# Reordering VectorE's and GpSimd's side work in the first pair of batches: gates ahead of conversion, weight sums in pieces, two weight matrices parked in DRAM

## The chip, the cores and the metric

The kernel runs on one core of a Trainium2 chip. The metric is the device time of the program in microseconds, from the median of several runs. All arithmetic is in fp32; the matmul engine is called TensorE or PE, the others VectorE (DVE), ScalarE (ACT), GpSimd (POOL) and SyncE (SP), which issues nearly all DMAs.

## The reference

```python
def _attn_ref(x, state):                # x (8, 8, 512, 64), state (8, 8, 32, 64)
    scores = scale * x @ state^T;  a = softmax(scores);   xread = a @ state
    scores2 = scale * state @ x^T; a2 = softmax(scores2); sread = a2 @ x
    return concatenate([xread, sread], axis=2)

def _moe_ref(x, w_in, w_out):           # x (4352, 512), w_in (512, 2048), w_out (2048, 512)
    h = x @ w_in
    g = h * np.cos(h)
    return g @ w_out

x = attn_out.transpose(0, 2, 1, 3).reshape(B * S, H * D)
```

There are eight batches. Each gives 512 token rows and 32 state rows to the second block. The two weight matrices arrive as float64, so the kernel converts them on the chip with integer operations.

## The kernel before, in words

The kernel walks through 80 **steps**; a step is one tile of 128 hidden columns of one batch (16 per batch), and the last 16 steps are the state rows of all batches. Two batches are a **pair** (32 steps, `PERIOD`). For a tile, TensorE makes the hidden values `h` in PSUM (`hidden`, L490); then comes the **gate** h*cos(h) in four parts: `gate` (ScalarE, L560, rounds h), `gate2` (VectorE, L563, the remainder), `gate3` (ScalarE, L566, the sine), `gate4` (VectorE, L580, the product, into a slot of `g_all`). In the first pair `h` has two PSUM buffers, so the matmuls of tile t+2 wait for `gate4` of tile t. The output product g @ w_out follows: for the first two rows of tiles plainly (L633), and for all others by a seven-product scheme on half matrices, two levels deep (L745), which needs sums of weights and sums of gated tiles.

`g_all` holds 12 **quads** of four tiles (128 x 2048 floats each) and a ring of four weight blocks. Quads 5 to 8 hold the four quarters A11, A12, A21, A22 of w_out, 9 to 11 are landing places of raw float64 data, quad 4 (`TEMPS`) takes GpSimd's temporaries. A quad whose content is used up goes to the list `quads_free`, and a tile or a sum takes one from its head.

What happens in the first pair beside the gates:

- **Conversion.** `convert(i, parts)` turns load i of 18 from float64 to fp32: "1" and "2" on ScalarE (L243, L246), "b" a shift on VectorE (L249), "c" an and/xor on VectorE (L252), "d" an add on GpSimd (L257), "f" fetches the next load. The table `conv_at` gives a step to each load; b, c, d follow one step later. The last load is finished in step 16. `e`, the exponents, lies in `aS_all`.
- **Weight sums.** For each of seven products the four quarters of a matrix are combined: `inner_weights` makes four sums on GpSimd (L671) and sends eight blocks of 256 KB to DRAM (`blocks_kept`). The matrices are A22, A11 and A12 themselves and four sums of them: SQ = A21+A22 (GpSimd), A21 = A11-A21 (VectorE), A22 = SQ-A11 (GpSimd) and SQ = A12-A22 (VectorE), all in L1092. Steps 15 to 27 hold this list, and A12 has its turn in step 50. Later, `fetch_block` on SP reads a block into the ring, three stages ahead of its use.
- **Outer sums.** Row2-row0 of the gated tiles goes to VectorE (L692), for this pair in steps 25 to 28.
- **Attention of the next batches**, placed by `plan(b)`: six lists per step (`pe`, `x_act`, `y_act`, `x_dve`, `y_dve`, `z_act`), which `go(0)` to `go(5)` issue at fixed places around the four parts of the gate.

The order on each engine is the order of the program, and every engine and the SP queue work in order. `first_pair` writes it out for steps 0 to 27, `later_pair` for the others. At the end of a step come the stores (`later`), `weights_at`, `outer_at` and `sums_at` of that step. In the later pairs tiles are gated two at a time (128x1024), and the hidden values of every token tile but those of the last quarter come from the seven-product scheme too: `sw_sums` (GpSimd, L523) and `halves` (VectorE, L509, into `aS_all`) prepare that.

Of the kernel before, what the change touches and what calls it, by code (L numbers as in the profile page):

```python
# [10 lines left out]
F32 = mybir.dt.float32  # L11
I32 = mybir.dt.int32
U32 = mybir.dt.uint32
ALU = mybir.AluOpType
# [8 lines left out]
def kernel(  # L23
# [8 lines left out]
    nc = tc.nc  # L32
# [4 lines left out]
    P = 128  # L37
# [38 lines left out]
    def quad(n):  # L76
        return g_all[:, QT * n:QT * n + QT]

    def matrix(n):
        return quad(n).rearrange("p t (u d) -> p (t u) d", d=HD)  # L80
# [6 lines left out]
            for i in range(NB)]  # L87
    spare = ctx.enter_context(tc.tile_pool(name="spare", bufs=1,
                                           space=bass.MemoryType.DRAM))
    blocks_kept = spare.tile([7, 8, P, QT * P], F32)  # L90

    xT = consts.tile([P, NK, S], F32)
    x_b = consts.tile([P, NC, H, D], F32)
# [170 lines left out]
    class Attention:  # L264
# [115 lines left out]
            self.exp2()  # L380

        def inverse(self, v):
            w = v.rearrange("p (a b) -> p b a", b=2)
            nc.vector.tensor_scalar(w, w, 1e-9, None, op0=ALU.add)
            nc.vector.reciprocal(v, v)
# [273 lines left out]
        m = m.rearrange("p (k i) (m d) -> p m k i d", k=2, m=2)  # L659
        return m[:, 0, 0], m[:, 0, 1], m[:, 1, 0], m[:, 1, 1]  # L660

    def inner_weights(which, m, temps=TEMPS):

        m11, m12, m21, m22 = quarters(m)
        t1, t2, t3, t4 = [quad(temps)[:, n].rearrange("p (i d) -> p i d", d=P)
                          for n in range(4)]
        for o, x1, x2, op in ((t1, m21, m22, ALU.add),
                              (t2, t1, m11, ALU.subtract),
                              (t3, m11, m21, ALU.subtract),
                              (t4, m12, t2, ALU.subtract)):  # L670
            nc.gpsimd.tensor_tensor(o, x1, x2, op=op)  # L671
        for n, block in enumerate((m11, m12, t4, m22, t1, t2, t3, m21)):
            nc.sync.dma_start(
                out=blocks_kept[which, n].rearrange("p (i d) -> p i d", d=P),
                in_=block)

    stage_list = []

# [279 lines left out]
    def plan(b):  # L958
# [12 lines left out]
        def early(b, s):  # L971
            if b == 1:
                pairs(s[0], b, "tokens", "tokens_kept", 0)
                pairs(s[1], b, "tokens", "tokens_kept", 2)
            else:
                for k in range(NK):
                    to = (x_dve, y_dve)[k % 2]
                    to[s[k // 2]].append((b, "tokens_turned", k))
            pe[s[2]].append((b, "scores"))
            x_dve[s[2]].append((b, "max1"))  # L980
            x_dve[s[3]].append((b, "spread1"))
            y_dve[s[3]].append((b, "shift"))
            if b == 1:
                x_dve[s[4]].append((b, "max2"))
                y_act[s[4]].append((b, "exps"))
            else:
                y_dve[s[4] - 1].append((b, "max2"))
                z_act[s[4]].append((b, "exps"))
            if b == 1:
                x_dve[s[5]].append((b, "sums"))  # L990
                y_dve[s[5]].append((b, "spread1"))
                x_dve[s[6]].append((b, "norm1"))
            else:
                y_dve[s[4]].append((b, "sums1"))
                x_dve[s[5]].append((b, "spread2"))
                y_dve[s[5]].append((b, "norm1"))

        def late(b, s):
            pairs(s[0], b, "turn", "turn_kept", 0)
            pe[s[1]].append((b, "reads", 0))  # L1000
            pe[s[2]].append((b, "reads", 1))
            x_dve[s[2]].append((b, "keep"))
            if len(s) > 3:
                turned(b, s[3])
# [65 lines left out]
    for n in range(B // 2):  # L1070
        end = n == B // 2 - 1
        for r, engine, o, x1, x2, half in (
                ((25, 26), dve, 0, 2, 0, 0), ((27, 28), dve, 0, 2, 0, 1),
                ((31, 31), pool, 2, 3, 2, 0), ((33, 33), dve, 0, 3, 0, 0),
                ((34, 34 + (not end)), dve, 0, 3, 0, 1),
                ((35, 36), dve, 2, 3, 2, 1),
                ((38 - end,) * 2, pool, 1, 1, 0, 0),
                ((39 - end,) * 2, pool, 1, 1, 0, 1)):
            for i in range(2):
                outer_at[PERIOD * n + r[i]].append(  # L1080
                    (engine, n, o, x1, x2, half, i))

# [2 lines left out]
                     for r in (o, x1, x2)]  # L1085
        sub(engine, o, x1, x2)

    def weight_sum(engine, o, x1, x2, op):
        n = 1 if engine is pool else 2
        for i in range(0, QT, n):  # L1090
            o_, x1_, x2_ = [quad(q)[:, i:i + n] for q in (o, x1, x2)]
            engine.tensor_tensor(o_, x1_, x2_, op=op)  # L1092

    def last_weights():
        temps = quads_free.pop(0)
        inner_weights(1, a12, temps)
        weights_at[53].append(lambda: quads_free.extend([A12, temps]))

    A11, A12, A21, A22, SQ = 5, 6, 7, 8, 11
    add_, sub_ = ALU.add, ALU.subtract  # L1100
    for at_, what in (
            (15, lambda: quads_free.append(10)),
            (16, lambda: inner_weights(2, a22)),
            (17, lambda: quads_free.append(9)),
            (17, lambda: weight_sum(pool, SQ, A21, A22, add_)),
            (18, lambda: inner_weights(3, matrix(SQ))),
            (18, lambda: weight_sum(dve, A21, A11, A21, sub_)),
            (19, lambda: inner_weights(0, a11)),
            (20, lambda: weight_sum(pool, A22, SQ, A11, sub_)),
            (21, lambda: inner_weights(5, matrix(A21))),  # L1110
            (22, lambda: inner_weights(4, matrix(A22))),
            (23, lambda: quads_free.append(A11)),
            (24, lambda: weight_sum(dve, SQ, A12, A22, sub_)),
            (25, lambda: quads_free.append(A21)),
            (25, lambda: inner_weights(6, matrix(SQ))),
            (27, lambda: quads_free.extend([A22, SQ, TEMPS])),
            (50, last_weights)):
        weights_at[at_].append(what)

    n_stages = 0  # L1120

# [17 lines left out]
    def first_pair(step, t):  # L1139
# [5 lines left out]
        if step == 0:  # L1145
            hidden(all_tiles[1])
            warm(3, acc[0])
            gate(t)
            gate2(t)
            convert(3, "bcdf")  # L1150
            convert(4, "1")
            go(0)
        else:
            go(0)
            if step == 5:
                states(1, side_banks[0])
            gate(t)
            gate2(t)
            if step == 3:
                warm(4, acc[0])  # L1160
                part(0, "products", 1, SIDE)
            go(1)
            go(3)
            if step == 1:
                convert(4, "bcdf")
            elif last >= 0:
                convert(last, "bcdf")
            if conv >= 0 and not todo[1]:
                convert(conv, "1")
        gate3(t)  # L1170
        go(5)
        if step == 3:
            part(0, "products_kept", 1, SIDE)
        gate4(t)
        if conv >= 0 and todo[1] and step > 0:
            convert(conv, "1")
        if step == 6:
# [129 lines left out]
```

## Time and profile before

| | before |
|---|---|
| median of 3 runs | 764.57 us (764.47 to 765.46) |
| span of the profiled run | 762.7 us |
| granted TensorE clock, mean | 0.990 |
| bytes read from and written to HBM | 87.03 and 23.59 MB |

The largest groups of the page, by engine (line, engine, operation, operands, count; busy us, mean ns; then idle time ahead of them and what ended most of it):

```profile
L692 POOL TENSOR_TENSOR g_all<-g_all 128x512 f32<-128x512 f32 x256 | 336.4, 1345 | 108.3 <-PE o L745 62.8
L745 PE MATMUL o<-g_all 128*128 128x256 f32 x1456 | 345.2, 382 | 4.4 <-POOL g_all L692 2.4
L490 PE MATMUL h<-aT,sw 128*128 128x512 f32 x224 | 108.8, 610 | 12.8 <-DVE g_all L580 12.1
L692 DVE TENSOR_TENSOR g_all<-g_all 128x1024 f32<-128x1024 f32 x40 | 56.7, 1433 | 0.1
L671 POOL TENSOR_TENSOR g_all<-g_all 128x512 f32<-128x512 f32 x28 | 37.7, 1371 | 12.2 <-DMA blocks_kept<-g_all 11.6
```

The mean of a pipelined matmul is longer than its share of the time: four 128x512 matmuls of one tile (L490) take 1.73 us from the start of the first to the start of what follows. The numbers of a row are sums over the whole run, so a row says how much there is, and the place is found in the timeline.

### The profile page before, as it was taken

To read this page: it belongs to the slowest core of one execution; us is meant where nothing else is said; L and a number is where in the kernel's file an instruction comes from. 1 tells how busy PE (TensorE), PEld (TensorE's weight loads), DVE (VectorE), ACT (ScalarE), POOL (GpSimd) and SP (SyncE) were. 2 spreads that over 40 slices of the span, in tenths; PEclk is the share of its full clock that TensorE was granted. 3 is DMA by queue.
4 is the path that set the end of the run, shared out by engine and by line. 5 is a ranking of instruction groups with operands and counts; after the bars stand their busy time and mean duration, and the time that the engine had idled before them with its cause. 6 is when DMAs were issued, how large, how long until landed. Compare 5 with 4: busy or idle time off the path is not lost.

```text
span 762.7 us, 10471 instructions
## 1 busy us (share of the span) xinstructions
PE 721.2 (95%) x3552; PEld 507.0 (66%) x3552; DVE 490.1 (64%) x683; ACT 330.9 (43%) x538; POOL 516.9 (68%) x480
## 2 busy tenths in 40 slices
PE   8998887779999999999999999999999999999998
PEld 3443322337777876677768876687778767888886
DVE  5768786783886757686866667759746446264650
ACT  3877962633454445434363445343634432211110
POOL 2344267779799895378998952479989534799600
PEclk9999998999999999999999999999999999999999
DMA  8495359679422685477225843672224456445661
GB/s 248 166 275 173 125 118 273 223 243 188 117 86 75 139 239 144 106 140 170 76 77 113 190 109 93 134 193 84 75 69 120 111 164 156 116 144 192 180 156 40
DMA packets 210356, 111.32 MB, mean 146 GB/s; under 512 B 158272, under 2 KB 173120, under 8 KB 210304
## 3 DMA queue, kind: packets, MB, share of 16 engines
q1 hardware_dynamic: 209216, 110.14, 55.3%
q8 instruction: 28, 0.46, 0.3%
q10 hardware_dynamic: 960, 0.39, 0.2%
q14 instruction: 24, 0.20, 0.1%
q0 software_dynamic: 128, 0.13, 0.1%
HBM read 87.03 MB, written 23.59 MB: 145 GB/s over the span
## 4 chain that ended last, share of the span: by engine, by line
PE 60%; POOL 20%; DVE 5%; DMA 5%; issue 4%; ACT 3%; SPq 1%; POOLq 0%; DVEq 0%; ACTq 0%
PE o L745 31%; POOL g_all L692 13%; PE h L490 10%; PE h L540 9%; POOL g_all L671 4%; PE at L328 3%; PE at L846 2%; DMA g_all<-blocks_kept 2%; POOL swS_all L523 2%; PE at L425 1%; DMA blocks_kept<-g_all 1%; POOL sw L523 1%; DMA x_b<-in_x_dram 1%; PE o L921 1%; PE o L846 1%
## 5 line engine op out<-in xcount | busy, mean ns | idle before, releaser
L692 POOL TENSOR_TENSOR g_all<-g_all 128x512 f32<-128x512 f32 x256 | 336.4, 1345 | 108.3 <-PE o L745 62.8
L745 PE MATMUL o<-g_all 128*128 128x256 f32 x1456 | 345.2, 382 | 4.4 <-POOL g_all L692 2.4
L745 PEld LDWEIGHTS o<-g_all 128*128 128x128 f32 x1456 | 273.9, 191 | 65.3 <-issue 19.2
L563 DVE TENSOR_TENSOR q_all<-q_all,h 128x1024 f32<-128x1024 int32 (+1 forms) x88 | 85.4, 970 | 58.7 <-ACT q_all L560 58.6
L490 PE MATMUL h<-aT,sw 128*128 128x512 f32 x224 | 108.8, 610 | 12.8 <-DVE g_all L580 12.1
L566 ACT ACTIVATE q_all<-q_all,halfpi 128x1024 f32<-128x1024 f32 (+1 forms) x88 | 84.3, 958 | 61.8 <-DVE q_all L563 61.7
L580 DVE TENSOR_TENSOR g_all<-h,q_all 128x1024 f32<-128x1024 f32 (+1 forms) x88 | 85.7, 974 | 34.6 <-ACT q_all L566 32.3
L560 ACT ACTIVATE q_all<-h 128x1024 int32<-128x1024 f32 (+1 forms) x88 | 73.5, 835 | 74.3 <-DVE g_all L580 32.3
L490 PEld LDWEIGHTS h<-aT,sw 128*128 128x128 f32 x224 | 41.5, 193 | 59.8 <-issue 32.1
L549 DVE TENSOR_TENSOR h<-h,sums_all 128x256 f32<-128x256 f32 x72 | 30.9, 429 | 63.7 <-PE h L540 49.0
L692 DVE TENSOR_TENSOR g_all<-g_all 128x1024 f32<-128x1024 f32 x40 | 56.7, 1433 | 0.1
L540 PE MATMUL h<-aS_all,swS_all 128*128 128x256 f32 x144 | 45.8, 400 | 7.3 <-POOL swS_all L523 5.5
L750 ACT COPY o<-o 128x256 f32<-128x256 f32 x26 | 9.3, 357 | 88.0 <-PE o L745 88.0
L540 PE MATMUL h<-aT,sw 128*128 128x256 f32 x144 | 44.7, 392 | 2.9 <-DVE g_all L580 2.5
L671 POOL TENSOR_TENSOR g_all<-g_all 128x512 f32<-128x512 f32 x28 | 37.7, 1371 | 12.2 <-DMA blocks_kept<-g_all 11.6
L257 POOL TENSOR_TENSOR w_in<-w_in,aS_all 128x1024 int32<-128x1024 int32 (+1 forms) x10 | 19.3, 1927 | 37.6 <-DVE w_in L252 22.3
L540 PE MATMUL h<-aS_all,sw 128*128 128x256 f32 x144 | 43.5, 384 | 0.0
L540 PEld LDWEIGHTS h<-aS_all,swS_all 128*128 128x128 f32 x144 | 25.5, 191 | 26.6 <-issue 7.8
L756 ACT COPY o<-sums_all 128x256 f32<-128x256 f32 x26 | 9.8, 378 | 74.0 <-PE o L745 74.0
L603 DVE SCALAR_TENSOR_TENSOR held<-o,held 128x512 f32<-128x512 f32 x40 | 27.1, 680 | 21.3 <-PE o L745 20.8
L461 ACT COPY sw<-at 128x512 f32<-128x512 f32 x50 | 26.8, 588 | 31.3 <-PE at L328 31.3
L257 POOL TENSOR_TENSOR g_all<-g_all,aS_all 128x1024 int32<-128x1024 int32 x8 | 18.9, 2363 | 29.3 <-DVE g_all L252 22.0
(112 smaller groups left out, 869.1 us busy)
## 6 DMA issues: line engine op xcount, KB each, us to landing
g_all<-blocks_kept SPq DMA_DIRECT2D x202, 256.0 KB, 2.8
blocks_kept<-g_all SPq DMA_DIRECT2D x56, 256.0 KB, 3.0
g_all<-in_moe_w_out_dram SPq DMA_DIRECT2D x8, 1024.0 KB, 5.1
out_dram<-ot SPq DMA_DIRECT2D x128, 64.0 KB, 2.0
g_all<-in_moe_w_in_dram SPq DMA_DIRECT2D x6, 1024.0 KB, 5.9
xT<-in_x_dram SPq DMA_DIRECT2D x96, 64.0 KB, 3.0
x_b<-in_x_dram SPq DMA_DIRECT2D x24, 256.0 KB, 4.9
x_b<-in_x_dram SPq DMA_DIRECT2D x16, 128.0 KB, 4.4
```

The source lines that it names most:

```text
L257: nc.gpsimd.tensor_tensor(bits, bits, e, op=ALU.add)
L490: nc.tensor.matmul(out=t.hp, lhsT=t.lhs(i), rhs=t.rhs(i), start=(i == 0), stop=(i == t.kn - 1))
L540: nc.tensor.matmul(out=out_, lhsT=w, rhs=r, start=start, stop=True, skip_group_check=True)
L549: nc.vector.tensor_tensor(o, h2[:, LO], sums_all[:, 0], op=ALU.add)
L560: nc.scalar.activation(t.q.bitcast(I32), t.hp, func=ACTF.Copy, bias=0.25)
L563: nc.vector.tensor_tensor(t.q, t.q.bitcast(I32), t.hp, op=ALU.subtract)
L566: nc.scalar.activation(t.q, t.q, func=ACTF.Sin, bias=halfpi, scale=-TWO_PI)
L580: nc.vector.tensor_tensor(g, t.hp, t.q, op=ALU.mult)
L603: nc.vector.scalar_tensor_tensor(out=out.t[:, ch], in0=bank, scalar=TWO_PI, in1=b.t[:, ch], op0=ALU.mult, op1=ALU.add)
L671: nc.gpsimd.tensor_tensor(o, x1, x2, op=op)
L692: engine.tensor_tensor(o[:, i:i + n], x1[:, i:i + n], x2[:, i:i + n], op=ALU.subtract)
L745: nc.tensor.matmul(out=o, lhsT=ring[(self.first + k) % NB][:, i], rhs=g[:, i], start=(start and i == 0), stop=(i == QT - 1), skip_group_ch ...
```

## The change

All of it concerns the first pair, except the two parked matrices.

1. In `first_pair`, `gate4` is issued ahead of the conversion: "b" stays ahead of `gate3` only where the step's `x_dve` list is empty, and "c", "d", "f" follow `gate4`.
2. The attention of batch 2 is spread: its maxima, exponentials, sums and normalisation are put one list or one step apart, and the second exponential comes one step after the first.
3. The sums row2-row0 of the first pair are made tile by tile (128x512) in steps 17 to 24, right after the tile, and VectorE's two weight sums are cut in four pieces each (steps 19 to 21 and 22 to 24).
4. The sums of A11 go to steps 9 to 12, one per step. GpSimd's temporaries have two homes, `TEMPS` and `aS_all`, in turns.
5. A22 (step 16) and A12 (step 22) are copied to DRAM (`kept`) and come back in steps 44 and 48 into a quad from the free list; their sums are made in steps 46 and 50. A12's quad is free from step 28 on. Before, A22 had its sums in step 16 and A12 held its quad to step 53.
6. The stores of `inner_weights` are put on `stores_due`, and so are issued at the head of the next step.

```diff
+    kept = spare.tile([2, P, QT * S], F32)
...
-        for n, block in enumerate((m11, m12, t4, m22, t1, t2, t3, m21)):
...
+        def send():
+            for n, block in enumerate((m11, m12, t4, m22, t1, t2, t3, m21)):
...
+        if 3 in pieces:
+            stores_due.append(send)
...
+            elif b == 2:
+                x_dve[s[4] - 1].append((b, "max2"))
+                z_act[s[4] - 1].append((b, "exp1"))
+                x_dve[s[4]].append((b, "sums1"))
+                z_act[s[4]].append((b, "exp2"))
+                x_dve[s[5]].append((b, "inverse", None))
+                y_dve[s[5]].append((b, "spread1"))
+                x_dve[s[5] + 1].append((b, "norm1"))
...
-                ((25, 26), dve, 0, 2, 0, 0), ((27, 28), dve, 0, 2, 0, 1),
+                (n and (25, 26), dve, 0, 2, 0, 0),
+                (n and (27, 28), dve, 0, 2, 0, 1), ((31, 31), pool, 2, 3, 2, 0), ((33, 33), dve, 0, 3, 0, 0),
...
+    def late_weights(step):
+        if step == 44:
+            late_quads.append(quads_free.pop(0))
+            move(late_quads[0], 0, False)
+        elif step == 46:
+            late_quads.append(quads_free.pop(0))
+        elif step == 48:
+            move(late_quads[0], 1, False)
+        elif step == 53:
+            quads_free.extend(late_quads)
+        if step in (46, 50):
+            q, temps = late_quads
+            inner_weights(2 if step == 46 else 1, matrix(q), quad(temps))
...
-            (16, lambda: inner_weights(2, a22)),
+            (16, lambda: move(A22, 0, True)),
...
-            (18, lambda: weight_sum(dve, A21, A11, A21, sub_)),
-            (19, lambda: inner_weights(0, a11)),
...
+            (22, lambda: move(A12, 1, True)),
...
-            (24, lambda: weight_sum(dve, SQ, A12, A22, sub_)),
...
+    for i in range(QT):
+        weights_at[9 + i].append(lambda i=i: inner_weights(
+            0, a11, temps[0], (i,)))
+        weights_at[(19, 20, 21, 21)[i]].append(lambda i=i: weight_sum(
+            dve, A21, A11, A21, sub_, (i,)))
+        weights_at[(22, 23, 24, 24)[i]].append(lambda i=i: weight_sum(
+            dve, SQ, A12, A22, sub_, (i,)))
+    for i in range(NH):
+        weights_at[17 + i].append(lambda i=i: first_outer_sum(i))
+    for step in (44, 46, 48, 50, 53):
+        weights_at[step].append(lambda step=step: late_weights(step))
...
-            if step == 1:
-                convert(4, "bcdf")
-            elif last >= 0:
-                convert(last, "bcdf")
+            if last >= 0 and not todo[3]:
+                convert(last, "b")
...
         gate4(t)
+        if last >= 0:
+            convert(last, "bcdf" if todo[3] else "cdf")
```

## The prediction

> **What bounds the kernel now.** I read the page first (who is busy), then the list of waits of the matmul queue (what it stands still for), then a table of engine time in stretches (where), and last the timeline around the largest waits (why).
>
> ```profile
> span 762.7 us, 10471 instructions
> PE 721.2 (95%) x3552; PEld 507.0 (66%) x3552; DVE 490.1 (64%) x683; ACT 330.9 (43%) x538; POOL 516.9 (68%) x480
> ...
> PE   8998887779999999999999999999999999999998
> ...
> POOL 2344267779799895378998952479989534799600
> PEclk9999998999999999999999999999999999999999
> DMA  8495359679422685477225843672224456445661
> ```
>
> TensorE is the bound: busy in tenths of 9 from slice 10 on (a slice is 19 us), and only the first ten slices, 0 to 190 us, have holes. That is the first pair of batches, steps 0 to 31. So a change there can win at most the holes, and a change in the second pair can win next to nothing but can lose. The waits of the matmuls between 20 and 190 us (us in total, times, longest):
>
> ```profile
> PE h L490 <- DVE g_all L580: 12.1, 9, 2.5
> PE at L328 <- DVE xT L310: 5.6, 1, 5.6
> PE h L540 <- POOL swS_all L523: 4.7, 1, 4.7
> PE o L745 <- DMA g_all<-blocks_kept: 1.3, 2, 0.9
> PE at L287 <- DMA x_b<-in_x_dram: 1.0, 2, 0.5
> ```
>
> Three causes carry 22.4 us: the gate product (L580) that releases the PSUM buffer of a tile two steps on, one long wait for a VectorE transpose, and one for GpSimd's weight sums. By stretches (stretch, length, then busy us of PE, PEld, DVE, ACT, POOL, granted clock, DMA share, GB/s):
>
> ```profile
> 80.00:100.00 20.00, 16.12 (x83) 7.34 (x82) 14.79 (x22) 17.78 (x24) 6.76 (x3) 1.00 0.50 130
> 100.00:120.00 20.00, 15.04 (x67) 4.89 (x65) 13.26 (x15) 7.85 (x13) 15.93 (x12) 1.00 0.52 133
> 120.00:140.00 20.00, 17.45 (x52) 5.96 (x52) 13.90 (x21) 8.50 (x13) 15.85 (x12) 0.83 0.92 253
> 140.00:160.00 20.00, 15.10 (x76) 6.66 (x76) 17.19 (x24) 10.00 (x18) 12.22 (x10) 0.91 0.67 213
> 160.00:180.00 20.00, 14.91 (x54) 9.76 (x47) 12.56 (x17) 5.61 (x12) 19.61 (x21) 0.91 0.88 220
> ```
>
> PE lacks 3.9, 5.0, 2.6, 4.9 and 5.1 us here, and its clock falls to 0.83 and 0.91: busy time is stretched as well. ACT is near full from 80 to 100 us, POOL from 100 on. The timeline shows the 5.6 us wait being made:
>
> ```profile
> 113.97 5.91 POOL L1092 TENSOR_TENSOR g_all<-g_all 128x512 f32<-128x512 f32 x4
> 116.50 2.27 DVE L1092 TENSOR_TENSOR g_all<-g_all 128x1024 f32<-128x1024 f32 x1 [3.87 <-POOL g_all L1092]
> 119.92 1.23 DVE L1092 TENSOR_TENSOR g_all<-g_all 128x1024 f32<-128x1024 f32 x1 [1.15 <-POOL g_all L1092]
> 121.66 0.70 DVE L310 STREAM_TRANSPOSE xT<-xT 128x512 f32<-128x512 f32 x1
> 122.42 3.46 PE L328 MATMUL at<-xT,st_all 64*32 64x512 f32 x8 [5.59 <-DVE xT L310]
> ```
>
> VectorE stands 3.87 and 1.15 us before the sum A11-A21 because GpSimd is still at A21+A22; behind it in VectorE's queue wait the gates of two tiles and the transpose that the scores need. The eight score matmuls then take 3.46 us; the eight before the hole took 1.06.
>
> [...] the sum above took 2.27 us beside GpSimd, and 1.23 where it had the start; the shift L249 took 1.83 and 1.94 us beside L257, 0.69 alone. [...]
>
> **The change part by part.**
>
> *Gate product ahead of conversion (steps 1 to 16).* No instruction is added. In a step whose VectorE list is empty the shift (0.69) stays ahead of the gate and the and/xor L252 (1.23) moves behind it; otherwise both move behind. Six waits for L580 lie there, at 74.7, 82.8, 93.1, 98.6, 102.8 and 107.1 us: 1.75, 0.53, 1.51, 1.83, 1.09, 0.61, together 7.3. The first goes (step 9: 1.9 us of conversion leaves a product that was awaited 1.75). The second is due to norm1 and stays. The other four sit where VectorE and ACT are both full (ACT 17.78 of 20): per step VectorE has gate 1.2, conversion 1.9, in step 14 also L435 1.2, and the shift now follows the previous and/xor by 0.6 us, so it falls more often on L257 (2.36 us), which cost 1.1 to 1.25 us twice already. I count 1.0 us won of the four. Sum: -2.75.
>
> *Sums in small pieces (steps 17 to 24).* Eight pieces of row2-row0 (before: four of 1024 at steps 25 to 28), four of A21 at 19 to 21 and four of SQ at 22 to 24 (before: two of 1024 each). GpSimd's A21+A22 now follows the conversions directly, since the sums of A22 left step 16 (5.09 us) and those of A11 moved to steps 9 to 12, where GpSimd has holes of 11.46 us; so the A21 pieces find it done and the 3.87+1.15 go. But these steps then carry all 16 pieces. VectorE per step without them, from starts of neighbours: gates 1.2 each, transposes 1.2 (steps 18, 19), L341 1.24 (20, 23), L347 1.17 and L362 1.19 (21), L357 1.2 (22), L384, L385 and L347 2.0 (24): 9.6+2.4+2.5+2.4+1.2+2.0 = 20.1. Pieces alone: 16 x 0.60 = 9.6. Sum 29.7. GpSimd is busy for nearly all of it (five groups of four at 5.1: 25.5, more with its own blocking), so each piece can be held. Lower bound 0.25 each (L692 on VectorE over the whole run averages 1433 ns against 1180 alone); upper bound what the held ones show in continuous GpSimd work, 0.25 to 1.05, mean about 0.7. I take 0.45: 7.2. VectorE needs 36.9 us, matmuls only 23.6 (8 tiles at 1.73, 4 second products at 1.73, scores and products about 3), so VectorE sets these steps. Before they took 137.99-102.82 = 35.2. So +1.7: the 5.6 us hole and its slow clock (3.0) are paid out again in smaller waits for L580.
>
> *Steps 25 to 28.* They lose 4.7 us of VectorE sums (1.17+1.17 of SQ in step 24's tail, 1.79, 1.44), and waits of 1.89 and 2.47 with 1.5 us of slow clock after them. Before: 160.07-137.99 = 22.1. After: the larger of PE and VectorE in each step: 4.3 (tile, second product, turn), 2.75, 4.5, 2.6: 14.2. The exps split over steps 22 and 23 add two table loads (1.28 each on ACT, which has room: 8.5 of 20), hidden but for 0.6 behind gate2. aS_all is now a home of temporaries: the halves of step 28 (L509) must wait until the stores of step 26 have read it; behind L509 stand the gates of tile 29. SP needs about 6 us for eight stores and 2.8 to land after GpSimd ends in step 25 or 26, about the three steps there are: 1.0. Sum 15.2: -6.9.
>
> *Two homes for temporaries, two matrices in DRAM: GpSimd's backlog at step 29.* GpSimd waited 11.6 us for stores of its one home and had ten more us of sums (A22, A11) in this stretch; the pair's sums start at 164.5 and swS at 170.75, for which PE waits 4.7 with some 1.7 of slow clock. All that is 20 us earlier now, and the pieces of SQ end in time. Of 7.1 us that PE lacks from 157.2 to 182 (24.8 less 17.7 of matmuls at full rate) I leave 1.5: -5.5.
>
> *Steps 44 to 53.* Added: two loads and two stores of 1 MB; four sums of A22 (5.1 us) at step 46, in a GpSimd that is 51.66 of 60 busy from 240 to 300 us. Idle there: 2.24, 0.68, 0.59, 3.34, so GpSimd is 4 to 5 us late until about 289. Waiting for it: swS, ready 3.3 to 4.6 us before its matmul, and the product sums, made one to two steps (4.7 each) ahead. That nearly hides it. On SP the stores of step 47 wait for the sums, eight of them take 6.07, and the second load waits for them; behind stand the block fetches, which run three stages (some 9 us) ahead and need 2.8. The existing group of this kind cost PE 0.73 at 291.8. Bounds 0 and 9 (three holds of 3 us); I take 1.5.
>
> Sum: -2.75+1.7-6.9-5.5+1.5 = -12.0. 764.6-12.0 = 752.6.
>
> **Rivals.**
> *No blocking (chance 0.20).* For it: VectorE's L249 and sums that start first are not slowed. Against: GpSimd is at 80% and more. Pieces at 0.60: steps 17 to 24 shrink by 7.2 more: 745.4.
> *The late sums are paid for (0.13).* For it: SP serves in order, and from 240 to 300 DMA is at 0.70 of its time. Against: the slack of the fetches. 9 instead of 1.5: 760.1.
> *Slower (0.09).* Pieces held for 1.0 each (+8.8) and the late sums at 9 (+7.5): 752.6+16.3 = 768.9. For it: VectorE is the full engine of steps 17 to 24 and gets more to do exactly there. [...]
> A remaining 0.03: all cancels, no change.
>
> **How the numbers follow.** Forecast 0.55, between 747 and 758 us; no blocking 0.20 (739 to 747); late sums 0.13 (758 to 763); slower 0.09; same 0.03. The range 742 to 761 holds the forecast, most of the two neighbours, and leaves out the ends. Faster 0.88, same 0.03, slower 0.09.
>
> **What would show it.** Right: the waits for L310 (5.6) and swS (4.7) gone; the first paired gate (L560, 128x1024), at 182.96 before, at about 169.5; clock 1.00 in the stretches from 120 to 180 but for one short dip; VectorE's 512 sums at 0.9 to 1.2 us mean; steps 46 to 54 (256.50 to 294.25, 37.75 us) 1 to 2 us longer. Wrong: the pieces at 0.7 mean (then the no-blocking rival), waits of PE for blocks_kept of several us between 240 and 300 (late sums), or L580 waits above 20 us before step 29.

## The result and the profile after

| | before | after |
|---|---|---|
| median | 764.71 us | 774.74 us (774.26 to 775.66, 4 runs) |
| ratio to before, 95% interval | 1 | 1.0131 (1.0113 to 1.0148) |
| span of the profiled run | 762.7 us | 773.8 us |
| granted TensorE clock, mean | 0.990 | 0.984 |

The change makes the kernel 1.3% slower; 752.6 us was forecast. (The median of before is that of its runs beside the changed kernel.) The page of the changed kernel, its rows of busy time and of slices of 19 us:

```profile
span 773.8 us, 10484 instructions
PE 723.6 (94%) x3552; PEld 507.3 (66%) x3552; DVE 496.0 (64%) x691; ACT 333.2 (43%) x540; POOL 518.7 (67%) x480
...
PE   8989848779999979999999999999999999999997
...
PEclk9999979899999999999999999999999999999999
```

TensorE has nearly as much to do as before (723.6 us against 721.2), so nearly all of the loss is waiting. The sixth slice (97 to 116 us) shows 4 in the PE row and 7 in the clock row, where before had 8 and 9: one large new hole. The 7 in the fifteenth slice (271 to 290 us), where before had 9, is a second one, in the second pair. (The 7 in the twenty-first slice brings no loss: from the gate of step 56 to the end, before takes 459.7 us and the changed kernel 460.5.) The waits of the matmuls from 20 to 190 us (us in total, times, longest), which answer to the list shown of before:

```profile
PE h L492 <- DVE g_all L582: 20.9, 10, 8.8
PE at L427 <- ACT xT L415: 3.8, 1, 3.8
...
PE o L635 <- POOL g_all L258: 0.9, 1, 0.9
```

The waits for L310 (5.6) and for `swS` (4.7), which the change was to remove, are gone but for 0.2 us. The wait for the gate product (now L582; 12.1 us before) is 20.9, with one single wait of 8.8, and a new one of 3.8 stands before the matmuls L427. The table by stretches (stretch, length, busy us of PE, PEld, DVE, ACT, POOL, granted clock, DMA share, GB/s) places them:

```profile
80.00:100.00 20.00, 16.95 (x84) 7.73 (x84) 15.36 (x22) 17.25 (x25) 8.93 (x5) 1.00 0.48 155
100.00:120.00 20.00, 10.36 (x35) 3.84 (x33) 12.90 (x14) 6.90 (x11) 8.17 (x4) 0.74 0.83 192
...
140.00:160.00 20.00, 11.98 (x40) 4.34 (x40) 17.01 (x24) 13.04 (x19) 11.39 (x9) 0.83 0.82 275
```

Between 100 and 120 us PE is busy for 10.36 us (15.04 before) at a clock of 0.74, and VectorE, ScalarE and GpSimd have 7 to 13 idle us of 20 each. All engines stand still together here, so I look for a transfer. The timeline there (start, length, engine, line, operands, and in brackets the idle time and its releaser) shows it whole:

```profile
90.79 7.65 SPq L678 DMA_DIRECT2D blocks_kept<-g_all  x8
98.56 0.59 SPq L213 DMA_DIRECT2D g_all<-in_moe_w_out_dram  x1
...
108.04 1.12 ACT L244 ACTIVATE g_all<-g_all 128x1024 f32<-128x1024 f32 x1 [8.31 <-DMA g_all<-in_moe_w_out_dram]
...
109.80 0.69 DVE L582 TENSOR_TENSOR g_all<-h,q_all 128x512 f32<-128x512 f32 x1 [6.31 <-ACT q_all L568]
110.54 3.71 PE L492 MATMUL h<-aT,sw 128*128 128x512 f32 x4 [8.80 <-DVE g_all L582]
```

Read it from the top. The eight stores of A11's sums go out at the head of step 13 and hold SP's queue for 7.65 us, 2.4 of them in a wait for the last sums. Behind them stands the fetch of the last piece of w_out. Its landing place is free when VectorE has read the piece before it, at 95.54 us (L253), but the fetch is issued at 98.56. It then takes 9.5 us to land. Before, it was the second of a group of two that starts at 87.96; it was issued at 92.5, and no fetch of this kind took more than 5.3 us. The fetches of w_out, before and after (duration of the issue in ns, first and last start in us; then issue to landing, shortest, median and longest):

```profile
L212 SPq DMA_DIRECT2D g_all<-in_moe_w_out_dram x8: 367/368/384, 27.2 to 92.5; - x8
DMA to landing us min/median/max: 4.9/5.1/5.3
...
L213 SPq DMA_DIRECT2D g_all<-in_moe_w_out_dram x8: 367/368/586, 27.1 to 98.6; - x8
DMA to landing us min/median/max: 4.9/5.0/9.5
```

ScalarE's first conversion instruction (L244), ahead of the sine of tile 15 in ScalarE's queue, waits 8.31 us for that piece; the product of tile 15 waits for the sine, the PSUM buffer for the product, PE for the buffer. The tile then takes 3.71 us at a granted clock of 0.53 (110.5 to 114.3 us), against 1.98 for a tile at a clock of 1.00 (135.6 to 137.6 us).

To see where the time goes, I compare the start of tiles on PE (of the gate at step 32 and later, where tiles are paired), not absolute times: the first gate starts between 24.58 and 26.07 us in the fourteen profiles, whatever the kernel.

| steps | before, us | after, us | difference | forecast |
|---|---|---|---|---|
| first gate to tile 9 | 41.10 | 42.72 | +1.6 | 0 |
| 9 to 17 | 36.97 | 43.18 | +6.2 | -2.75 |
| 17 to 25 | 35.17 | 38.38 | +3.2 | +1.7 |
| 25 to 29 | 22.08 | 22.15 | +0.1 | -6.9 |
| 29 to 32 | 22.89 | 16.32 | -6.6 | -5.5 |
| 32 to 46 | 73.54 | 72.31 | -1.2 | 0 |
| 46 to 56 | 46.48 | 53.64 | +7.2 | +1.5 |

The sum is +10.5; the medians differ by 10.0. The last row is the parked matrices, seen here in the timeline of the changed kernel:

```profile
267.79 6.44 SPq L678 DMA_DIRECT2D blocks_kept<-g_all  x8
274.33 0.68 SPq L691 DMA_DIRECT2D g_all<-blocks_kept  x1
...
278.43 3.39 PE L753 MATMUL o<-g_all 128*128 128x256 f32 x8 [2.99 <-DMA g_all<-blocks_kept]
```

A block that PE needs (L691) is issued behind eight stores; PE waits 2.99 us for it and then works slowly, 3.39 us for eight matmuls where 1.99 is usual (the granted clock is 0.50 from 278 to 280 us). Over the run PE's wait for blocks is 4.6 us in three pieces.

### The profile page after: what moved, and what is told of

Read it like the earlier page. It is cut to its first block, busy times and chain, and to the rows that moved or that the text cites. A ratio compares the mean times of both kernels' runs of the same rounds, so it can differ in the third digit from the quotient of the medians.

```text
span 773.8 us, 10484 instructions
## 1 busy us (share of the span) xinstructions
PE 723.6 (94%) x3552; PEld 507.3 (66%) x3552; DVE 496.0 (64%) x691; ACT 333.2 (43%) x540; POOL 518.7 (67%) x480
## 4 chain that ended last, share of the span: by engine, by line
PE 56%; POOL 22%; DVE 7%; DMA 4%; ACT 4%; issue 4%; SPq 2%; POOLq 0%; DVEq 0%; ACTq 0%
PE o L753 29%; POOL g_all L700 14%; PE h L492 10%; PE h L542 8%; PE at L329 2%; POOL swS_all L525 2%; PE at L854 2%; SPq L132 2%; PE at L427 1%; POOL sw L525 1%; POOL g_all L1110 1%; DMA x_b<-in_x_dram 1%; DVE q_all L565 1%; POOL g_all L674 1%; ACT q_all L568 1%
## 5 line engine op out<-in xcount | busy, mean ns | idle before, releaser
L700 POOL TENSOR_TENSOR g_all<-g_all 128x512 f32<-128x512 f32 x256 | 335.2, 1346 | 103.0 <-PE o L753 57.6
L492 PE MATMUL h<-aT,sw 128*128 128x512 f32 x224 | 112.4, 626 | 21.5 <-DVE g_all L582 20.9
L582 DVE TENSOR_TENSOR g_all<-h,q_all 128x1024 f32<-128x1024 f32 (+1 forms) x88 | 85.6, 973 | 41.2 <-ACT q_all L568 40.3
L492 PEld LDWEIGHTS h<-aT,sw 128*128 128x128 f32 x224 | 42.3, 197 | 69.5 <-issue 34.8
L700 DVE TENSOR_TENSOR g_all<-g_all 128x1024 f32<-128x1024 f32 x36 | 50.2, 1410 | 0.1
L258 POOL TENSOR_TENSOR w_in<-w_in,aS_all 128x1024 int32<-128x1024 int32 (+1 forms) x10 | 19.2, 1925 | 39.3 <-DVE w_in L253 26.3
L258 POOL TENSOR_TENSOR g_all<-g_all,aS_all 128x1024 int32<-128x1024 int32 x8 | 18.9, 2361 | 32.1 <-DVE g_all L253 30.9
L542 PEld LDWEIGHTS h<-aT,sw 128*128 128x128 f32 x144 | 25.9, 189 | 12.5 <-DVE g_all L582 9.3
```

The lines of the kernel that those rows point to most:

```text
L258: nc.gpsimd.tensor_tensor(bits, bits, e, op=ALU.add)
L492: nc.tensor.matmul(out=t.hp, lhsT=t.lhs(i), rhs=t.rhs(i), start=(i == 0), stop=(i == t.kn - 1))
L542: nc.tensor.matmul(out=out_, lhsT=w, rhs=r, start=start, stop=True, skip_group_check=True)
L582: nc.vector.tensor_tensor(g, t.hp, t.q, op=ALU.mult)
L700: engine.tensor_tensor(o[:, i:i + n], x1[:, i:i + n], x2[:, i:i + n], op=ALU.subtract)
```

## The experiments

The theory after this reading had four parts, each with a rival: the order in SP's queue at step 13 (A of e1), the parked matrices (in the second pair), the new plan of batch 2 (C), and the new gate order. Twelve kernels were run. "vs before" is the ratio of times on the same chip with its 95% interval; the medians of before on the four occasions were 766.28, 765.65, 765.65 and 766.31 us.

| kernel | median, us | vs before |
|---|---|---|
| e1 load ahead of A11's stores | 770.14 | 1.0052 (1.0037 to 1.0067) |
| e2 nothing parked | 767.75 | 1.0018 (1.0010 to 1.0025) |
| e3 old plan of batch 2 | 774.33 | 1.0116 (1.0088 to 1.0143) |
| e4 old gate order | 772.44 | 1.0080 (1.0062 to 1.0097) |
| f1 = e1 + e2 | 763.39 | 0.9963 (0.9950 to 0.9976) |
| f2 = f1 + e4 | 761.07 | 0.9938 (0.9916 to 0.9960) |
| f3 = f2 + e3 | 760.61 | 0.9920 (0.9897 to 0.9942) |
| f4 late stores spread | 772.06 | 1.0078 (1.0048 to 1.0108) |
| g1 = f3, outer sums back in steps 25 to 28 | 759.63 | 0.9925 (0.9897 to 0.9953) |
| g2 = f3, one home for temporaries | 762.86 | 0.9963 (0.9951 to 0.9974) |
| h1 no reload | 776.94 | 1.0141 (1.0108 to 1.0174) |
| h2 late stores on ScalarE's queue | 785.13 | 1.0244 (1.0206 to 1.0282) |

The same stretches as above, for those that the argument uses (us):

| steps | before | after | e1 | e3 | f1 | f2 | f3 | g1 | g2 |
|---|---|---|---|---|---|---|---|---|---|
| first gate to 9 | 41.10 | 42.72 | 42.79 | 42.55 | 43.09 | 41.18 | 41.10 | 41.82 | 40.96 |
| 9 to 17 | 36.97 | 43.18 | 36.37 | 41.90 | 36.33 | 37.74 | 37.72 | 37.76 | 37.74 |
| 17 to 25 | 35.17 | 38.38 | 37.25 | 39.40 | 38.31 | 37.20 | 38.12 | 31.98 | 39.36 |
| 25 to 29 | 22.08 | 22.15 | 22.31 | 20.02 | 23.08 | 22.34 | 20.03 | 20.33 | 23.00 |
| 29 to 32 | 22.89 | 16.32 | 16.32 | 16.32 | 16.31 | 16.30 | 16.31 | 24.06 | 16.30 |
| 46 to 56 | 46.48 | 53.64 | 53.56 | 54.33 | 47.52 | 47.09 | 46.73 | 47.28 | 47.18 |

Each column is one profile. How far one row can be trusted shows where the code is the same: the six profiles with A11's stores in step 13 and the new gate order take 41.60 to 43.18 us from tile 9 to tile 17.

### e1: the load ahead of the stores

```diff
-        if 3 in pieces:
+        if 3 in pieces and which == 0:
+            weights_at[15].append(lambda: stores_due.append(send))
+        elif 3 in pieces:
             stores_due.append(send)
```

> The changed kernel, but the eight stores of A11's sums leave at the head of step 16 instead of step 13, so that the fetch of the last piece of w_out stands ahead of them in SP's queue. Theory A (queue: the last piece comes late because 2 MB of stores go first, and ScalarE waits for it ahead of a sine): ScalarE's wait of 8.3 us ahead of L244 falls below 1 us, the gates of steps 15 to 17 come 6 to 9 us earlier, 765.5 to 768.5 us. Theory B (VectorE is the limit here because small sums and shifts are held by GpSimd): the piece was not what ended the wait, 773 to 775.

Measured: 770.14 us, 1.0052, against 1.0131 for the whole change. Only A11's stores moved (to the head of step 16). ScalarE's wait for the load falls from 8.3 to 1.5 us, and steps 9 to 17 take 36.37 us instead of 43.18 (or instead of 41.60, the shortest of the six). So the stores ahead of the load are the cause of that row, 5 to 7 us; by the ratios the kernel gains 6.0, less than A gave, and far more than B.

The order in SP's queue is only one half of it. Here the fetch goes out 0.1 us after VectorE has read the piece before it, at 97.0 us, and takes 5.6 us to land; in the changed kernel it goes out 3.0 us after that and takes 9.5. So of the 6.8 us some 3.0 are standing behind the stores in the queue, and some 3.9 a slower landing while the DMA engines still carry them (their share from 92 to 98 us is 1.02 in the changed kernel and 0.45 here). e1 takes both away at once; no run takes away one alone.

### e2: nothing parked

```diff
-        if step == 44:
-            late_quads.append(quads_free.pop(0))
-            move(late_quads[0], 0, False)
...
+        if step == 50:
+            late_quads.extend([A12, quads_free.pop(0)])
+            inner_weights(1, a12, quad(late_quads[1]))
...
-            (16, lambda: move(A22, 0, True)),
+            (16, lambda: inner_weights(2, a22, temps[0])),
...
-            (22, lambda: move(A12, 1, True)),
...
```

> The changed kernel without the two parked matrices: A22 has its sums in step 16 again, A12 holds its quad until step 53 and has its sums in step 50, as before the change. Theory A (SP's queue in steps 44 to 53: loads and stores of parked matrices ahead of block fetches): the 7.2 us lost between the gates of steps 46 and 56 go away to within 1 us; the sums of A22 cost GpSimd 5.1 us again in steps 16 to 18, of which 0 to 5 us reach TensorE: 767.5 to 772.5. Theory B (GpSimd's additional 5 us are the loss wherever they stand): what is won after step 46 is lost in steps 16 to 24, 774 to 776.

Measured: 767.75 us, at the low end of what A expected. Steps 46 to 56 give back 6.6 us, PE's wait for blocks is 1.3 us instead of 4.6, and the first pair is not longer for A22's four sums in step 16: the gate of step 29 even comes 1.7 us earlier, nearly all of it ahead of tile 17, where the two kernels have the same code. The parking costs what the table says and brings nothing that the traces show.

### e3: the old plan of batch 2

```diff
-            elif b == 2:
-                x_dve[s[4] - 1].append((b, "max2"))
-                z_act[s[4] - 1].append((b, "exp1"))
...
-                x_dve[s[5] + 1].append((b, "norm1"))
             else:
...
-            if b == 2:
-                x_act[s[0]].remove((b, "turn_kept", 0))
-                y_act[s[0]].insert(0, (b, "turn_kept", 0))
```

> The changed kernel with the attention of batch 2 planned as before the change (exponentials together in step 23, norm1 in step 24, first turn_kept in x_act). Theory C (the reads of step 26 wait 3.8 us for turn_kept because it now follows norm1 in step 25): this wait goes, the gates of steps 25 to 29 come 3 to 6 us closer, 769 to 772. Rival (VectorE is late in steps 20 to 24 anyhow, so all that comes after it is late under either plan, and the exponentials in one piece hold ScalarE for 4.3 us again): 774 to 777.

Measured: 774.33 us, inside the rival's range; the interval overlaps that of the whole change. The profile shows two effects that nearly cancel. The new wait of PE (L427) is gone, and steps 25 to 29 take 20.02 us instead of 22.15. Steps 17 to 25 take 39.40 instead of 38.38. How the wait is made, in the changed kernel:

```profile
158.34 1.69 DVE L404 TENSOR_TENSOR aT<-aT,xT 128x1024 f32<-128x1024 f32 x1
...
160.12 1.07 ACT L415 COPY xT<-at 128x512 f32<-128x512 f32 x2 [0.94 <-DVE aT L404]
160.76 1.09 PE L427 MATMUL at<-x_b,xT 128*64 128x128 f32 x16 [3.83 <-ACT xT L415]
```

The normalisation L404 (`norm1`) now comes in the step in which PE reads its result, behind a transpose, three pieces and a remainder on VectorE (3.5 us, from 154.81 to 158.34): the plan took away all slack between them.

### e4: the old gate order

```diff
-            if last >= 0 and not todo[3]:
-                convert(last, "b")
+            if step == 1:
+                convert(4, "bcdf")
+            elif last >= 0:
+                convert(last, "bcdf")
...
         gate4(t)
-        if last >= 0:
-            convert(last, "bcdf" if todo[3] else "cdf")
```

> The changed kernel with the conversion ahead of the gate product again. As forecast (the order wins 2.75 us in steps 9 to 17): 776.5 to 778.5. Rival (in steps 1 to 8 TensorE sets the pace and the order only makes the conversion late, for which the first products wait, 1.8 us; in steps 9 to 16 ScalarE and VectorE are full under either order): 772 to 775. If the fetch of the last piece of w_out, which follows the conversion, also comes earlier, up to 2 us less.

Measured: 772.44 us, in the rival's range: undoing the part that was to win 2.75 us makes the kernel faster. Part of this is a shorter wait for the last piece of w_out (5.9 us instead of 8.3). The stretch to tile 9 takes 42.5 to 43.1 us in the eight kernels with the new order, and 41.0 to 41.8 in the six with the old one, before among them.

### f1, f2, f3: undone together

f1 joins e1 and e2 (A22's sums use the second home), f2 adds e4, f3 adds e3; the edits are those above.

> The changed kernel with both repairs: the stores of A11's sums follow the fetch of the last piece of w_out (step 16), and no matrix is parked (A22's sums in step 16, with aS_all as their home; A12 resident to step 53). If the two losses are separate, the ratio to before is 1.0131 less 0.0079 and 0.0113, near 0.994: 759 to 762 us at 765 of before. If they overlap (the same SP queue or the same GpSimd time is freed twice), 763 to 767.

Measured: 763.39 us. By the ratios e1 and e2 win 0.79 and 1.13 points alone and 1.68 together, where they would win 1.92 if they were separate. Most of each is its own. A little overlap, as the rival had it, is possible but not shown: the missing 0.24 points are less than the four intervals allow for.

> As f1_first_and_resident, and the conversion ahead of the gate product again. If the gate order itself costs 2 us, as the gates of steps 4 to 9 show in e4_old_gate (the rest of its gain there being the shorter wait for the last piece of w_out), 2 us less than f1. Rival: with the last piece early, VectorE's waits in steps 12 to 16 are worth 2.75 us as forecast, and this kernel is 1 us or more slower than f1.

Measured: 761.07 us. With the queue in order the gate order can be read by itself: the old one is 1.9 us shorter to tile 9 (41.18 against 43.09) and 1.4 us longer from 9 to 17 (37.74 against 36.33). There the new order does win; before tile 9 it loses more. The medians differ by 2.3 us, but the two intervals overlap.

> As f2_and_old_gate, and batch 2's attention planned as before the change. What is left of the change: sums in small pieces and earlier, A11's sums in steps 9 to 12, two homes, stores one step late. e3_old_plan2 won 2.2 us up to step 29: 1 to 3 us less than f2, near 0.989 of before. Rival (ScalarE's 4.3 us of exponentials in one step count once VectorE is less late): the same as f2 or up to 2 us more.

Measured: 760.61 us, 0.9920 of before. f2 and f3 can't be told apart by their medians; in the profiles, the gate of step 29 comes 1.5 us sooner after the first gate in f3 (139.05 against 140.54). f3 beats before by 0.8% and the whole change by about 2%. It keeps the sums in pieces, the early outer sums, the two homes and A11's early sums.

### g1 and g2: what of f3 brings the gain

```diff
-                (n and (25, 26), dve, 0, 2, 0, 0),
-                (n and (27, 28), dve, 0, 2, 0, 1), ((31, 31), pool, 2, 3, 2, 0), ((33, 33), dve, 0, 3, 0, 0),
+                ((25, 26), dve, 0, 2, 0, 0), ((27, 28), dve, 0, 2, 0, 1),
+                ((31, 31), pool, 2, 3, 2, 0), ((33, 33), dve, 0, 3, 0, 0),
...
-    for i in range(NH):
-        weights_at[17 + i].append(lambda i=i: first_outer_sum(i))
```

> As f3_and_old_plan2, with the eight sums row2-row0 back in steps 25 to 28 as four of 128x1024. If VectorE's extra work in steps 17 to 24 costs what it lasts there (eight pieces at about 1.3 us held by GpSimd, less what is hidden), steps 17 to 25 become 4 to 8 us shorter and steps 25 to 29 3 to 5 us longer, where GpSimd waits and VectorE has room: 0 to 4 us less than f3. Rival (the pieces fill holes of VectorE, and the four large ones meet GpSimd in steps 25 to 28 as before the change): 1 to 4 us more than f3.

Measured: 759.63 us, 0.9925: the same as f3. But inside nothing is the same: steps 17 to 25 are 6.1 us shorter than in f3, and 29 to 32 are 7.8 longer, near the 22.89 of before. Steps 25 to 29, expected 3 to 5 longer, hardly move (20.33 against 20.03). (The rows of the table are from one run each; that of g1 had a span of 760.5 us, that of f3 757.1, so they don't cancel in full.) Two lines of g1 say why (GpSimd's product sum, and PE's second product):

```profile
163.04 1.31 POOL L702 TENSOR_TENSOR g_all<-g_all 128x512 f32<-128x512 f32 x1 [3.77 <-DVE g_all L702]
...
171.33 3.78 PE L755 MATMUL o<-g_all 128*128 128x256 f32 x8 [2.97 <-ACT sums_all L761]
```

With the outer sums in steps 25 to 28, GpSimd waits for them (3.77 us and, earlier, 1.33) with the sums of the pair, and PE for `swS` (1.36) and for ScalarE (2.97). So the short stretch 29 to 32 is bought by the early outer sums and paid for in steps 17 to 25.

```diff
-            (16, lambda: inner_weights(2, a22, temps[1])),
+            (16, lambda: inner_weights(2, a22, temps[0])),
...
-            (21, lambda: inner_weights(4, matrix(A22), temps[1])),
+            (21, lambda: inner_weights(4, matrix(A22), temps[0])),
...
-            (25, lambda: inner_weights(6, matrix(SQ), temps[1])),
+            (25, lambda: inner_weights(6, matrix(SQ), temps[0])),
```

> As f3_and_old_plan2, but all of GpSimd's temporaries in TEMPS. If the second home is what brings GpSimd's sums in ahead of step 29 (before the change GpSimd waited 11.6 us for stores out of its one home), GpSimd waits 8 to 12 us for stores again between steps 16 and 26, and the pair ends 3 to 6 us later: 764 to 767. Rival (the early sums of A11 and the shorter waits give slack enough, and GpSimd stands 7 us for VectorE's last pieces of SQ anyhow): within 1.5 us of f3.

Measured: 762.86 us, by the ratios 3.3 us more than f3 (0.9963 against 0.9920, the intervals apart) and between the two ranges. GpSimd waits for stores again, 10.4 us in four waits:

```profile
POOL g_all L674 <- DMA blocks_kept<-g_all: 10.4, 4, 3.9
```

It costs 1.2 us in steps 17 to 25 and 3.0 in 25 to 29, and nothing in 29 to 32. A11's early sums and the pieces of VectorE's weight sums were not taken back in any run, so their share of f3's gain is not shown.

### f4, h1, h2: what in the parking delays the blocks

Three readings were open: the eight stores hold the SP queue in one piece (A1), the DMA engines have too much to do at all (A2), or GpSimd is late because it waits for the reload (A3).

```diff
+        if 3 in pieces and which in (1, 2):
+            n = 8 // len(SPREAD[which])
+            for i, at_ in enumerate(SPREAD[which]):
+                weights_at[at_].append(lambda i=i: stores_due.append(
+                    lambda: send(n * i, n * i + n)))
...
+    SPREAD = {2: (46, 47, 48, 49), 1: (52, 53)}
...
-        elif step == 48:
+        elif step == 50:
             move(late_quads[0], 1, False)
...
-        if step in (46, 50):
+        if step in (46, 52):
```

> The changed kernel with its parked matrices, but the eight stores of A22's sums leave two per step in steps 47 to 50, A12 is loaded in step 50, its sums are made in step 52 and leave four per step in 53 and 54. Theory A1 (block fetches stand behind eight stores in SP's queue): TensorE's waits for blocks_kept between 255 and 310 us fall from 4.6 us to under 1.5, 768 to 771. Theory A2 (the DMA engines are full, with 4 MB more in these steps, and the order in the queue does not matter): waits of 3 us or more remain, 772 to 775.

Measured: 772.06 us, just inside A2's range, though the profile speaks for A1 in half: steps 46 to 56 take 49.93 us, so 3.5 of the 7.2 are lost instead of all. (A12's load and sums come two steps later here, so the half is not the spread stores' alone.) One wait of PE for blocks is left:

```profile
PE o L762 <- DMA g_all<-blocks_kept: 2.2, 1, 2.2
```

Ahead of that block in the queue there still stand two stores and four loads of x (4.31 us), and SP is busy nearly without a break from 266.7 to 281 us. Whether the remainder is order or load isn't settled.

```diff
         if step == 44:
             late_quads.append(quads_free.pop(0))
-            move(late_quads[0], 0, False)
         elif step == 46:
             late_quads.append(quads_free.pop(0))
-        elif step == 48:
-            move(late_quads[0], 1, False)
...
```

> The changed kernel, but A22 and A12 are not loaded back: the sums of steps 46 and 50 are made from whatever their quad holds, so the blocks of two of the seven weight sets are not those of the reference; all other work is the same. Theory A1 (block fetches stand behind the eight stores in SP's queue): TensorE's waits for blocks_kept between 255 and 310 us stay at 3 us or more, 772 to 775. Theory A3 (the two loads of 1 MB, or GpSimd's wait of 8.4 us for the second of them, are what is paid for): these waits fall below 1.5 us, 766 to 769.

Measured: 776.94 us, above both ranges and no better than the whole change (1.0141 against 1.0131, intervals overlap). GpSimd no longer waits 8.4 us for the second reload, yet steps 46 to 56 take 53.56 us, as in the changed kernel, and PE waits 5.8 us for blocks. A3 falls: neither the reload's 2 MB nor GpSimd's wait for it is the cause. It also speaks against A2: the mean share of the DMA engines from 256 to 296 us is 0.86 here, near the 0.84 of before (0.95 in the changed kernel), and the loss stays.

```diff
+            queue = nc.scalar if which in (1, 2) else nc.sync
             for n, block in enumerate((m11, m12, t4, m22, t1, t2, t3, m21)):
-                nc.sync.dma_start(
+                queue.dma_start(
```

> The changed kernel, but the sixteen stores of the two parked matrices' sums are issued from ScalarE's queue instead of SP's; the same bytes move at about the same time. Theory A1 (SP's queue): TensorE's waits for blocks_kept between 255 and 310 us fall below 1.5 us; ScalarE waits for GpSimd's sums instead and gets up to 6 us of issue per group, of which some reaches the gates: 768 to 773. Theory A2 (the DMA engines are full): the waits stay at 3 us or more, 773 to 778.

Measured: 785.13 us, far above both. The experiment made a new wait larger than the one studied. ScalarE's queue, with its next gate (start, length, idle):

```profile
261.08 8.51 ACTq L679 DMA_DIRECT2D blocks_kept<-g_all  x8
269.64 1.15 ACT L568 ACTIVATE q_all<-q_all,halfpi 128x1024 f32<-128x1024 f32 x1 [8.25 <-DMA blocks_kept<-g_all]
```

ScalarE computes nothing while its queue works through the stores and waits for GpSimd's last sums, which end at 264.9 us (8.25 us, and 6.61 for the second group), and PE waits 3.98 and 5.47 us for gate products. PE's wait for blocks only falls from 4.6 to 3.1. It decides nothing between A1 and A2.

## Why the prediction was wrong

**Gate product ahead of conversion (-2.75, measured +6.2 in steps 9 to 17 and +1.6 before).** This is the step that failed worst, and its failure has two parts. The larger one is not in the gate at all: the change puts A11's sums in steps 9 to 12, "where GpSimd has holes", as the prediction says in its part on the small sums; there it asked only whether GpSimd has room. It put at nothing what the 2 MB of stores behind them do to the load that follows them, in SP's queue and on the DMA engines, although it named SP's order for the late sums. e1 alone removes 5 to 7 us of it. What is left in steps 9 to 17 (36.37 in e1) is 0.6 under before, and the order of the gate itself wins 1.4 there (f1 against f2): the right sign and half the size. Against it stands the stretch to tile 9, which the prediction put at nothing: all conversion moves later by a gate product, PE's first output product waits 0.9 us for GpSimd's add (L258), and the eight kernels with this order take 1.4 to 2.0 us longer there than before. Net, the edit costs half a microsecond up to tile 17 (f1 against f2); the medians of the two differ by 2.3, with intervals that overlap.

**Sums in small pieces (+1.7, measured +3.2).** The mechanism was right and the size nearly so: 36.9 us were forecast for steps 17 to 25, 38.38 measured. The sixteen pieces took 18.3 us, 1.14 each. Eight of them took 0.65 to 0.68 and the other eight 1.06 to 1.81; on the mean a piece was held 0.5 us, where 0.45 was taken. All eight long ones ran beside instructions of GpSimd; three of its own sums that overlap two of them (136.87 to 141.8 us) lasted 1.59 to 1.71 us, the next one 1.27. The rival "No blocking" falls by this: cutting the sums into pieces did not end the blocking.

**Steps 25 to 28 (-6.9, measured +0.1).** The sum took "the larger of PE and VectorE in each step". That was the error. In f3, which has the old plan of batch 2, neither is full in these steps (PE 16.84 of 20 us, VectorE 14.96), and PE waits 1.15 and 2.01 us there for gate products:

```profile
142.00:162.00 20.00, 16.84 (x81) 7.42 (x81) 14.96 (x26) 11.91 (x21) 12.93 (x11) 0.91 0.88 287
```

A gate goes through ScalarE, VectorE, ScalarE and VectorE in turn, and with two PSUM buffers the matmuls of a tile wait for the gate two tiles back. So I read the length of a step as that chain plus whatever stands between its parts on either queue; no run tests this reading by itself. The spread plan of batch 2 put things in between: two more table loads (1.28 us each), which the prediction called hidden but for 0.6 (one stands ahead of a sine, and its product on VectorE idles 1.81 us), and a normalisation that PE awaits for 3.83. With the old plan (f3) the stretch is 20.03 us, still 4.8 above the 15.2 forecast. g1, which has three of the outer sums in these very steps (1.78, 1.45 and 1.22 us), takes 20.33: taking them out did not shorten the steps. (The sums that the prediction lists here make 5.6 us, not the 4.7 that it names.)

**GpSimd's backlog at step 29 (-5.5, measured -6.6).** The size was right, the reason only half. g2, with one home, loses 4.2 us before step 29 but keeps the short stretch 29 to 32; g1, with two homes, loses the short stretch. It is the early outer sums that shorten steps 29 to 32, and the second home that helps in 17 to 29.

**Steps 44 to 53 (+1.5, measured +7.2).** The bounds of 0 and 9 held it, the value taken didn't. The prediction had named the mechanism (block fetches behind eight stores on SP) and trusted the lead of some 9 us of the fetches. It counted 6.07 us for eight stores and 2.8 for the landing, together just inside that lead. Here the stores hold the queue for 6.44 us, and from the issue of the block behind them to PE's start on it there are 4.1 (274.33 to 278.43). The hold of 2.99 us also has slow matmuls after it, 3.39 us instead of 1.99 at a granted clock of 0.50 (278 to 280 us) and 0.67 (280 to 282); one of 0.84 us had not (1.99). The clock is the second part of the price of this hole.

Of the tests named, the waits for L310 and `swS` went as said, and the pieces' mean of 1.14 us lay in the 0.9 to 1.2 given; the gate of step 32 came at 187.39, not 169.5; the clock from 120 to 180 us was 1.00, 0.83 and 0.91, with more than one short dip. Two of the signs of being wrong came: waits for `blocks_kept` of several us, and more than 20 us of waits for the gate product before step 29 (20.9). Of the rivals, "The late sums are paid for" came true (+7.2 of at most +9). "Slower" had the direction and, with the late sums, one of its two reasons; its other, pieces held for 1.0 us each, did not come. No rival had the load behind A11's stores.

One reading of the prediction needs a correction: it gave the hole of 5.6 us a slow clock worth 3.0 us, but the 3.46 us of the eight score matmuls (1.06 before the hole) are not the clock alone. A single one took 1.06 us instead of 0.60, at a granted clock of 0.50 (122 to 126 us), and the second four also had to wait for a second transpose (L310, done at 123.84 us).

The parts of the loss that the runs show are two of 6 to 9 us each by the ratios (the stores ahead of the load at step 13, the parking) and a small one for the gate order. Together they are more than the 10 us lost, since the rest of the change gains: with them taken back (f1 to f3) it is 0.4 to 0.8% faster than before. Not settled: how the loss at step 13 would split if the queue alone were put right, how the remainder in f4 splits between order and load, and whether f3's last step brings anything.

## What to carry to other kernels

When work moves to where an engine has room, follow its outputs and the queue that carries them: here eight stores that were issued earlier put off the load behind them in the same queue by 3.0 us, it took 9.5 us to land instead of 5.6, and this one late load stopped all engines in turn (PE for 8.80 us). Where a loop runs through several engines with two buffers, don't price a step by its fullest engine (15.2 us forecast for steps 25 to 28, 20.03 in f3) but by the chain through all of them, with what stands in between. And a stretch that becomes shorter is no proof for the part that was meant to shorten it: g1 and f3 have the same time with 6 to 8 us distributed differently.

## What the runs showed of the hardware

- Eight stores of 256 KB held the SP queue for 6.44 us, 0.8 us each, and for 7.65 us with 2.4 in a wait for their sums; in before's group it was 6.07.
- A load of 1 MB of w_out issued right behind such a group took 9.5 us to land; without the group ahead it took 5.6 (e1), and the eight of before took 4.9 to 5.3.
- VectorE's sixteen sums of 128x512 took 1.06 to 1.81 us in eight cases, all of them beside an instruction of GpSimd, and 0.65 to 0.68 in the others.
- A group of eight stores on ScalarE's queue stopped its arithmetic for 8.25 us, part of it a wait for GpSimd's sums; the same group held SP for 6.44.
- A hole of 8.80 us cost more than itself: the next tile took 3.71 us and not 1.98, at a granted clock of 0.53 (0.74 in that stretch of 20 us). Shorter holes did not act alike: after one of 2.62 us a tile took 1.98 us in the changed kernel and in e4, 2.55 in f4, 2.58 in e3 and 3.22 in e1.
- The first gate starts up to 1.5 us earlier or later in profiles of kernels whose code up to there is the same, so stretches were compared, not moments.
